# A block-sorted attention feeding a squared-ReLU network: regrouped sorting in the first batch, crossbar transposes for half of the second, and a planner with new due times, new load times and slack behind DMAs

## The chip, the core and the metric

The kernel runs on one core of a Trainium2 chip. The metric is the device time of one execution in microseconds (us), on that one core.

TensorE multiplies matrices, VectorE and ScalarE do elementwise work and empty TensorE's accumulators (PSUM), GpSimd and Sync mostly issue DMAs here. Five instruction streams run side by side and wait for one another by semaphores.

## The reference

Attention over blocks: a softmaxed 8 x 8 matrix P for each head mixes ("sorts") the 8 blocks of keys and values, then each query block attends to its own sorted block of 96 rows. The result, transposed to tokens by features, goes through a two-layer network with squared ReLU.

```python
# batch, heads, seq, head_dim, blocks = 4, 8, 768, 64, 8;  3072 tokens, d_model 512, d_ff 2048
P = sort_net
for _ in range(5):                      # exp, then normalise over rows and columns
    ...
k_sorted = np.einsum('bhij,bhjcd->bhicd', P, k_b).reshape(B, H, S, D)
v_sorted = np.einsum('bhij,bhjcd->bhicd', P, v_b).reshape(B, H, S, D)
...
scores = scale * np.matmul(q_b, k_sb.transpose(0, 1, 2, 4, 3))   # within a block
...                                                              # softmax
attn_out = np.matmul(attn, v_sb).reshape(B, H, S, D)
x = attn_out.transpose(0, 2, 1, 3).reshape(B * S, H * D)
h = np.maximum(x @ w_in, 0.0)
out = h * h @ w_out
```

## The kernel before

The network's matmuls (512 up-projections of 384 columns, 368 down-projections of 512, and a last tile cut in smaller pieces) fill TensorE. The attention of batch b+1 is slipped between the matmuls of batch b. The eight heads of a batch are worked in four pairs.

There are two ways to attention. **On TensorE**: q is transposed by TensorE, k (and in the first batch v) is sorted and transposed in one go by matmuls with a 128-wide expansion of P (`w_all`), and scores are read from `ksT`. **By crossbar DMA**: P is applied in natural layout by quarter-array matmuls (32 x 32, weights `w_t`), VectorE or ScalarE evicts the sorted keys to `kn` in bf16, VectorE copies q, which is bf16 already, to `qi` in another order, and two transposing DMAs on the Sync queue turn them into `kx` and `qT`. Sorted values go out to a DRAM buffer (`v_way`) and come back as `vblk` in the layout that attention-times-values wants. Before the change the first and second batch took the first way for keys and the third and fourth the second; values go by `v_way` from the second batch on.

The order of all instructions is found when the program is built. A planner simulates the engines with a fixed cost for each operation, lets an attention group go ahead of the network's matmuls once its **due time** (counted in chunks of four network matmuls) has come, and emits instructions in the order of the simulated start times. Its estimates never run on the chip; what they fix is the *order* in each engine's queue.

```python
class Plan:
    TAIL = {"PE": 0.0, "ACT": 0.09, "DVE": 0.06, "POOL": 0.0, "DMA": 0.0, "SP": 0.0, "WAY": 0.6}
    HOP = 0.06
    SWITCH = 0.1
    ...
    def ready(self, op):
        if any(d.end is None for d in op.deps):
            return None
        return max([d.end + self.HOP for d in op.deps], default=0.0)
```

"DMA" stands for the loads, whose estimated time is their megabytes over a rate; "WAY" for transfers issued by Sync (the value round trip and the transposes).

```python
    def dma(key, mb, dst_src, deps=()):
        ...
        op = plan.add("POOL", 0.75, issue, deps)
        landed[key] = plan.add("DMA", mb / (0.39 if key[0] == 0 else 0.43), lambda e: None, [op, landed.get("last")])
        landed["last"] = landed[key]
...
    def s_nat(b, g, t, due):            # sort two pairs in natural layout, t = 1 keys, 2 values
        ...
        wr = plan.add("SP", 0.33, write, evs + ([loaded(b)] if b > 1 else []))    # v_way <- vn
        slow = 6.0 if b == 1 else 2.0
        there = plan.add("WAY", slow, lambda e: None, [wr])
        rd = plan.add("SP", 0.33, read, [there] + oldw)                           # vblk <- v_way
        back = plan.add("WAY", slow, lambda e: None, [rd])
...
    def loaded(b):
        return landed[b, 0, HP, 0]      # the last q half of batch b
```

A store of the result is no operation of its own in the plan: it is emitted with the copy that it waits for, so the plan doesn't know that it holds the Sync queue until that copy is done.

```python
            def store(e, mt=mt):
                ob = ffn.tile([128, d_model], FP32, tag="ob", name="ob", bufs=3)
                copy(e, ob, t["op", mt])
                nc.sync.dma_start(out=out[t0 + 128 * mt:t0 + 128 * (mt + 1), :], in_=ob)

            op = plan.add(AD, cost_f(d_model), store, [pe])
```

The softmax here doesn't subtract the row's maximum and nothing guards it: scores larger than these inputs give would overflow.

## Time and profile before

| | before |
|---|---|
| time, median of 3 runs | 226.1 us (226.03 to 226.43) |
| span of the profiled run | 224.2 us, clock 1.0 |
| TensorE busy | 97% |
| VectorE, ScalarE busy | 46%, 54% |
| first up-projection starts | 22.13 us |
| last matmul group ends | 220.29 us |

TensorE sets the time, so the reading is a sum along TensorE: when the network starts, how much work there is, how many changes of array layout, and what is lost in waits. The prediction below does this sum. Three lines from the list of waits: engine, tile and line, then what ended the wait, the total in us, how often, and the longest.

```profile
DVE qi L708 <- DMA qb<-in_q_dram: 7.9, 2, 6.6
...
DVE kn L194 <- DMA kx<-kn: 5.0, 1, 5.0
...
DVE qi L708 <- DMA qT<-qi: 3.1, 2, 2.7
```

VectorE stood 7.9 us before q copies whose load had not landed, and 8.1 us before `kn` and `qi` buffers that a transpose had not freed. A line of a timeline gives start, duration, operation, destination and source, count. The second is the Sync queue's timeline in the fourth batch (start, duration, operation, destination and source, count):

```profile
126.61 3.79 SPq L867 DMA_DIRECT2D out_dram<-ob  x2
141.67 0.38 SPq L668 DMA_DIRECT2D v_way<-vn  x1
142.14 1.66 SPq L696 DMA_TRANSPOSE kx<-kn  x1
143.85 1.39 SPq L719 DMA_TRANSPOSE qT<-qi  x1
145.44 0.43 SPq L867 DMA_DIRECT2D out_dram<-ob  x1
146.53 0.33 SPq L674 DMA_DIRECT2D vblk<-v_way  x1
```

The values are written at 141.67 and read back from 146.53, and the next store comes after the write.

### The profile page before, as it was taken

What the parts mean: (1) busy time and instruction counts of PE and PEld (TensorE: products, weight loads), DVE (VectorE), ACT (ScalarE), POOL (GpSimd) and SP (SyncE); (2) the same over time, 40 slices, a digit from 0 to 9 for tenths busy, and PEclk for the clock granted to TensorE, in tenths of its full rate; (3) what the DMA queues carried; (4) which work ended last, traced back from release to release, by engine and by line L of the source; (5) the groups of instructions that cost most, each with busy time, mean ns of one, the idle gap of its engine ahead of it and who ended that gap; (6) DMA issues with size and microseconds to landing.
All of it is one profiled execution on the core that took longest, in us unless ns stands there. A gap on an engine that the chain in (4) does not pass through costs nothing.

```text
span 224.2 us, 5181 instructions
## 1 busy us (share of the span) xinstructions
PE 216.7 (97%) x2097; PEld 120.5 (54%) x2097; DVE 102.6 (46%) x300; ACT 120.4 (54%) x252; POOL 26.6 (12%) x49
## 2 busy tenths in 40 slices
PE   8998999999999999999999999999999999999993
PEld 2576655546665555445665454436665465456562
DVE  6777777422575416530663236332663255015300
ACT  4666677418985138445765178336772276147421
POOL 7972320000001500000000150000000000000000
PEclk9999999999999999999999999999999999999999
DMA  5999999999221899997922489999843310120012
GB/s 73 202 203 206 208 206 212 209 230 268 59 38 35 146 241 210 137 230 186 144 59 38 129 139 229 198 226 237 192 39 82 83 50 0 47 94 3 0 68 72
DMA packets 43767, 30.43 MB, mean 136 GB/s; under 512 B 22816, under 2 KB 38944, under 8 KB 43744
## 3 DMA queue, kind: packets, MB, share of 16 engines
q0 software_dynamic: 13120, 13.63, 37.3%
q1 hardware_dynamic: 30624, 16.48, 34.0%
q8 instruction: 16, 0.26, 0.5%
q14 instruction: 7, 0.06, 0.1%
HBM read 29.70 MB, written 8.72 MB: 171 GB/s over the span
## 4 chain that ended last, share of the span: by engine, by line
PE 64%; DMA 13%; DVE 9%; issue 5%; ACT 4%; POOL 2%; POOLq 0%; SPq 0%; ACTq 0%; DVEq 0%
PE hp L823 27%; PE op L851 24%; DMA qb<-in_q_dram 8%; DVE ao L755 3%; PE p L561 3%; DMA xT<-ao 3%; PE p L744 2%; DMA kx<-kn 2%; ACT h L831 2%; PE op L885 2%; PE p L644 1%; PE p L518 1%; ACT et L593 1%; PE vbp L609 1%; PE tp L518 1%
## 5 line engine op out<-in xcount | busy, mean ns | idle before, releaser
L823 PE MATMUL hp<-xT,w_in_bf 128*128 128x384 bf16 x512 | 90.7, 327 | 0.5 <-ACT h L831 0.5
L851 PE MATMUL op<-w_out_bf,h 128*128 128x512 bf16 x368 | 83.6, 379 | 0.0
L831 ACT ACTIVATE h<-hp 128x384 bf16<-128x384 f32 x128 | 60.6, 497 | 22.1 <-PE hp L823 15.2
L834 DVE TENSOR_TENSOR h<-h 128x384 bf16<-128x384 bf16 x128 | 43.7, 354 | 54.9 <-ACT h L831 54.0
L823 PEld LDWEIGHTS <-w_in_bf 128*128 128x128 bf16 x512 | 47.2, 97 | 31.6 <-issue 1.4
L851 PEld LDWEIGHTS <-h 128*128 128x128 bf16 x368 | 34.5, 98 | 39.3 <-issue 0.7
L192 ACT COPY ob<-op 128x512 f32<-128x512 f32 (+1 forms) x23 | 13.0, 567 | 58.3 <-PE op L851 52.8
L755 DVE TENSOR_TENSOR ao<-p,rec 96x512 bf16<-96x512 f32 x32 | 22.0, 686 | 1.1
L593 ACT ACTIVATE et<-p 96x384 bf16<-96x384 f32 x48 | 19.5, 492 | 4.8 <-PE p L561 4.8
L744 PEld LDWEIGHTS <-et 96*128 96x128 bf16 x256 | 10.7, 97 | 2.8 <-ACT et L584 0.2
L754 DVE RECIPROCAL rec<-p 96x8 f32<-96x8 f32 x32 | 6.3, 198 | 10.7 <-PE p L744 9.3
L998 POOL COPY held<-xT 1x3 bf16<-1x3 bf16 (+1 forms) x2 | 0.4, 183 | 91.3 <-DMA xT<-ao 91.3
L357 PE MATMUL p<-ones 128*128 128x512 bf16 (+1 forms) x36 | 9.8, 395 | 1.1 <-DVE ones L213 1.1
L744 PE MATMUL p<-vblk,et 96*128 96x65 bf16 x192 | 8.3, 193 | 0.0
L194 DVE CAST kn<-p 128x768 bf16<-128x768 f32 x4 | 3.8, 957 | 8.8 <-DMA kx<-kn 5.0
L708 DVE COPY qi<-qb 128x768 bf16<-128x768 bf16 x8 | 2.7, 355 | 11.0 <-DMA qb<-in_q_dram 7.9
L194 DVE CAST vn<-p 128x768 bf16<-128x768 f32 x6 | 5.7, 957 | 3.3 <-PE p L644 3.3
L264 POOL DMA_DIRECT2D kb<-in_k_dram x10 | 6.6, 662 | 3.6 <-DMA w_in_bf<-in_moe_w_in_dram 2.0
L264 POOL DMA_DIRECT2D qb<-in_q_dram x8 | 6.1, 767 | 4.6 <-DMA w_in_bf<-in_moe_w_in_dram 1.9
L584 ACT ACTIVATE et<-p 96x768 bf16<-96x768 f32 x8 | 6.3, 802 | 0.6 <-PE p L561 0.5
L264 POOL DMA_DIRECT2D vb<-in_v_dram x10 | 6.3, 634 | 2.0 <-DMA w_in_bf<-in_moe_w_in_dram 2.0
L561 PEld LDWEIGHTS <-kx 64*128 64x128 bf16 x128 | 4.6, 155 | 2.9 <-issue 2.9
(81 smaller groups left out, 126.5 us busy)
## 6 DMA issues: line engine op xcount, KB each, us to landing
out_dram<-ob SPq DMA_DIRECT2D x23, 256.0 KB, 3.3
qb<-in_q_dram POOLq DMA_DIRECT2D x8, 384.0 KB, 11.7
v_way<-vn SPq DMA_DIRECT2D x6, 396.0 KB, 5.0
vblk<-v_way SPq DMA_DIRECT2D x6, 396.0 KB, 4.3
vb<-in_v_dram POOLq DMA_DIRECT2D x6, 384.0 KB, 12.5
kb<-in_k_dram POOLq DMA_DIRECT2D x6, 384.0 KB, 10.4
w_in_bf<-in_moe_w_in_dram POOLq DMA_DIRECT2D x4, 512.0 KB, 11.7
w_out_bf<-in_moe_w_out_dram POOLq DMA_DIRECT2D x4, 512.0 KB, 18.8
```

Of the source, the lines that this page charges most:

```text
L192: nc.scalar.copy(out=out, in_=in_)
L194: nc.vector.tensor_copy(out=out, in_=in_)
L264: nc.gpsimd.dma_start(out=dst, in_=src)
L357: nc.tensor.matmul(out=out, lhsT=ones, rhs=rhs, start=True, stop=True)
L561: nc.tensor.matmul(out=scp[:, h, BLK * n:BLK * (n + 1)], lhsT=(u.ksT[64 * h:64 * (h + 1), HS * hf + BLK * n:HS * hf + BLK * n + 128] if u. ...
L593: nc.scalar.activation(out=et[:, h, 0:HS].rearrange("p (n c a) -> p n c a", c=C0, a=NA), in_=st["p"][0:96, h, 0:HS].rearrange("p (n a c) - ...
L744: nc.tensor.matmul(out=oup[:, h, 66 * n:66 * n + D + 1], lhsT=et_r[u.et[hf]][:, h, BLK * n:BLK * n + 128], rhs=(u.vs[:, NQ * hf + n, h, 0: ...
L755: nc.vector.tensor_tensor(out=u.ao[:, n0:n0 + NQ, :, :].rearrange("p n e d -> p e n d"), in0=ov[:, :, :, 0:D], in1=rec[:, :, :, None].to_b ...
L823: nc.tensor.matmul(out=t["hp", nt][:, 0:HS], lhsT=w_in_bf[:, kc, 128 * nt:128 * (nt + 1)], rhs=xT[:, kc, t0:t0 + HS], start=(kc == 0), sto ...
L831: nc.scalar.activation(out=t["h1", nt], in_=t["hp", nt][:, 0:HS], func=AF.Relu)
L834: nc.vector.tensor_tensor(out=t["h2"][:, nt, :], in0=t["h1", nt], in1=t["h1", nt], op=ALU.mult)
L851: nc.tensor.matmul(out=t["op", mt], lhsT=t["h2"][:, nt, 128 * mt:128 * (mt + 1)], rhs=w_out_bf[:, nt, :], start=(nt == 0), stop=(nt == NT ...
```

## The change

Its intent: less TensorE work in the second batch, fewer changes of array layout in the first, and q copies that no longer block VectorE.

1. In the second batch, pairs 2 and 3 take the crossbar way; pairs 0 and 1 stay on TensorE.
2. In the first batch's second half, one function sorts keys and values of a pair into one PSUM tile, with one wide eviction, and due times bring two pairs at a time.
3. Due times of all stages come from a search (table `DUES`) in place of formulas. The planner gets new load times (`rate`, and 4.5 us in place of 3.2 after the hold), 2.5 us of slack behind every load and 1.0 behind every Sync transfer after 45 us ("late landings"), and four `kn` and four `qi` buffers in place of three and two.

```diff
+DUES = {
+    (0, "K"): (-15.0, -1.0, 10, 10),
+    (0, "S"): (-1.0, 11.0, 11.0, 15.0),
 ...
+    (3, "A"): (149.5, 155.0, 160.5, 162.5),
+    (3, "X"): (158.5, 160.0, 161.5, 166.5),
+}
 ...
+    SLACK = {"DMA": 2.5, "WAY": 1.0}
 ...
-        return max([d.end + self.HOP for d in op.deps], default=0.0)
+        late = op.engs[0] not in self.SLACK
+        return max([d.end + self.HOP + (self.SLACK.get(d.eng, 0.0) if late and d.end > 45 else 0.0)
+                    for d in op.deps], default=0.0)
 ...
-    rkx, rkn, rqi = Ring(3), Ring(3), Ring(2)
+    rkx, rkn, rqi = Ring(3), Ring(4), Ring(4)
 ...
-        landed[key] = plan.add("DMA", mb / (0.39 if key[0] == 0 else 0.43), lambda e: None, [op, landed.get("last")])
+        landed[key] = plan.add("DMA", mb / (0.39 if key[0] == 0 else 0.43 if long else rate), lambda e: None, [op, landed.get("last")])
 ...
+    def in_tiles(b, t, h0):
+        return b > 1 and t > 0 or b == 1 and t == 2 or b == 1 and t == 1 and h0 == HP
 ...
+            b < 2 and (b < 1 or in_tiles(b, t, h0)), 0.23 if b == 1 else 0.37 if t else 0.29)
 ...
+    def s_sort2(u, due):
+        ...                       # keys and values of a pair into one PSUM tile
+        u.k_op = u.v_op = plan.add(AD, cost_f(2 * n), ev, pes + u.old)
 ...
-        landed["last"] = plan.add("DMA", 3.2, lambda e: None, [holds[b]])
+        landed["last"] = plan.add("DMA", 4.5, lambda e: None, [holds[b]])
```

More of the change, by code (lines that the diff above doesn't have):

```diff
@@ L13 @@
 AX = mybir.AxisListType
+DUES = {
+    (0, "K"): (-15.0, -1.0, 10, 10),
+    (0, "S"): (-1.0, 11.0, 11.0, 15.0),
+    (0, "T"): (-1.5, 10.0, 13.5, 19.5),
+    (0, "A"): (14.0, 14.5, 18.0, 21.5),
+    (0, "X"): (16.0, 23.0, 24.5, 25.0),
+    (0, "W"): (1.5,),
+    (1, "V"): (4.0, 20.5),
+    (1, "Q"): (31.0,),
+    (1, "N"): (None, 33.0),
+    (1, "Z"): (None, None, 43.0, 44.0),
+    (1, "S"): (33.5, 41.0, 43.0, 48.0),
+    (1, "A"): (39.5, 41.5, 45.5, 52.0),
+    (1, "X"): (48.0, 49.5, 49.5, 55.0),
+    (2, "L"): (52.0,),
+    (2, "N"): (64.0, 69.5),
+    (2, "V"): (74.5, 91.5),
+    (2, "Z"): (84.0, 86.0, 95.5, 96.5),
+    (2, "S"): (88.5, 93.0, 97.5, 100.5),
+    (2, "A"): (95.0, 99.5, 102.0, 104.0),
+    (2, "X"): (96.5, 105.5, 107.5, 109.5),
+    (3, "L"): (110.5,),
+    (3, "N"): (120.0, 126.0),
+    (3, "V"): (123.0, 141.5),
+    (3, "Z"): (130.5, 138.0, 153.0, 155.5),
+    (3, "S"): (143.5, 153.0, 157.5, 159.5),
+    (3, "A"): (149.5, 155.0, 160.5, 162.5),
+    (3, "X"): (158.5, 160.0, 161.5, 166.5),
+}
 FIRST = ("K0 V0 K1 v1 S0 t0 S1 k2 t1 A0 V2 S2 K3 t2 A1 V3 X0 A2 S3 t3 x1 A3 X2 x3")
@@ L215 @@
     nc.vector.memset(ident, 0.0)
-    ksT_r, vsT_r, et_r, vs_r = [], [], [], []
+    kvT_r, et_r, vs_r = [], [], []
     for n in range(3):
-        for r, name in ((ksT_r, "ksT"), (vsT_r, "vsT")):
-            sT = const.tile([128, S + 32], BF16, name=f"{name}{n}")
-            for x in (HS, S):
-                nc.vector.memset(sT[:, x:x + 32], 0.0)
-            r.append(sT)
+        sT = const.tile([128, 2, S + 32], BF16, name=f"kvT{n}")
+        for x in (HS, S):
+            nc.vector.memset(sT[:, :, x:x + 32], 0.0)
+        kvT_r.append(sT)
         vs = const.tile([96, NB, 2, 66], BF16, name=f"vs{n}")
@@ L236 @@
     v_way = nc.dram_tensor("v_way", (B, 2, NA, 128, HP * 66), BF16, kind="Internal").ap()
-    kn_r = [const.tile([128, NA, 2, D], BF16, name=f"kn{n}") for n in range(3)]
-    qi_r = [const.tile([128, NA, 2, D], BF16, name=f"qi{n}") for n in range(2)]
+    kn_r = [const.tile([128, NA, 2, D], BF16, name=f"kn{n}") for n in range(4)]
+    qi_r = [const.tile([128, NA, 2, D], BF16, name=f"qi{n}") for n in range(4)]
     kx_r = []
@@ L259, with dma @@
     landed = {}
-    def dma(key, mb, dst_src, deps=()):
+    def dma(key, mb, dst_src, deps=(), long=True, rate=0.23):
         def issue(e):
@@ L277, in dst_src @@
             alloc_qkv(b)
-            if b > 1 and t or b == 1 and t == 2:
+            if in_tiles(b, t, h0):
                 return (qkv[b][t].rearrange("p (g h) x -> p g (h x)", h=HP)[:, h0 // HP, :],
@@ L282, in load @@
         dma((b, t, h0, p.start), 1.57 * n / H * (p.stop - p.start) / 128, dst_src,
-            readers[b - 2] + [holds[b]] if b > 1 else [])
+            readers[b - 2] + [holds[b]] if b > 1 else [],
+            b < 2 and (b < 1 or in_tiles(b, t, h0)), 0.23 if b == 1 else 0.37 if t else 0.29)
     def load_w_in(g):
@@ L444, in __init__ @@
             self.b, self.hp, self.halves = b, hp, halves
-            if b > 1:
+            self.tiled = in_tiles(b, 1, HP * (hp // 2))
+            if self.tiled:
                 self.i0, self.ni, self.full = 0, NB, True
@@ L448, in __init__ @@
             self.n, self.old = rks.take()
-            self.ksT, self.vsT, self.vs = ksT_r[self.n], vsT_r[self.n], vs_r[self.n]
+            self.kvT, self.vs = kvT_r[self.n], vs_r[self.n]
+            self.ksT, self.vsT = self.kvT[:, 0, :], self.kvT[:, 1, :]
             self.i0, self.ni = NQ * halves[0], NQ * len(halves)
@@ L543, in s_sort, with mm, ev @@
         return op
+    def s_sort2(u, due):
+        st = {}
+        s2, old = r2.take()
+        n = NA * u.ni * C0
+        def mm(e, t):
+            for a in range(NA):
+                for h in range(2):
+                    nc.tensor.matmul(
+                        out=p2[s2][64 * h:64 * (h + 1), t - 1, u.ni * C0 * a:u.ni * C0 * (a + 1)],
+                        lhsT=qkv[u.b][t][:, 2 * u.hp + h, D * a:D * (a + 1)],
+                        rhs=w_all[:, H * u.b + 2 * u.hp + h, u.i0:u.i0 + u.ni, :]
+                        .rearrange("p i c -> p (i c)"),
+                        start=True, stop=True)
+        def ev(e):
+            copy(e, u.kvT[:, :, BLK * u.i0:BLK * (u.i0 + u.ni)]
+                 .rearrange("p t (x a) -> p t x a", a=NA),
+                 p2[s2][:, :, 0:n].rearrange("p t (a x) -> p t x a", a=NA))
+        pes = [plan.add("PE", 0.2, lambda e, t=t: mm(e, t),
+                        [landed[u.b, t, 2 * u.hp, 0], built[H * u.b + 2 * u.hp],
+                         built[H * u.b + 2 * u.hp + 1]] + old, due, mode="col") for t in (1, 2)]
+        readers[u.b] += pes
+        u.k_op = u.v_op = plan.add(AD, cost_f(2 * n), ev, pes + u.old)
+        r2.use(s2, *pes, u.k_op)
     def s_sc(u, due=0):
@@ L555, in mm @@
                 qT = tiles["qT", u.b, u.hp]
-                if u.b < 2:
+                if not u.tiled:
                     qT = qT.rearrange("p a x -> p (a x)").rearrange("p (i q) -> p i q", q=BLK)
@@ L563, in mm @@
                             lhsT=(u.ksT[64 * h:64 * (h + 1), HS * hf + BLK * n:HS * hf + BLK * n + 128]
-                                  if u.b < 2 else
+                                  if not u.tiled else
                                   kx_r[u.kx][64 * h:64 * (h + 1), NQ * hf + n::NB]),
-                            rhs=(qT[64 * h:64 * (h + 1), NQ * hf + n, :] if u.b < 2 else
+                            rhs=(qT[64 * h:64 * (h + 1), NQ * hf + n, :] if not u.tiled else
                                  qT[64 * h:64 * (h + 1), :, C0 * (NQ * hf + n):
@@ L572, in s_sc @@
             u.et[hf], olde = ret.take()
-            pe = plan.add("PE", 0.17 if u.b < 2 else 0.26, mm, [u.k_op, u.q_op] + old, due,
+            pe = plan.add("PE", 0.17 if not u.tiled else 0.26, mm, [u.k_op, u.q_op] + old, due,
                           mode="row")
@@ L576, in s_sc @@
             rqT.use(qTs[u.b, u.hp], pe)
-            if u.b < 2:
+            if not u.tiled:
                 rks.use(u.n, pe)
@@ L946 @@
     todo = []
-    kops = {}
-    def lay(b, halves, c0, c1):
-        step, gap = (c1 - c0) / (HP + 0.9), (c1 - c0 - 13) / (HP - 1)
-        for hp in range(HP):
-            c = c0 + step * hp
-            box = {}
-            def open_(due, b=b, hp=hp, box=box):
-                u = box["u"] = Unit(b, hp, halves)
-                u.q_op = q2ops[hp] if b == 0 else s_q(b, hp, 0, 128, due)
-                if b == 1:
-                    build_w(H * b + 2 * hp, 2, pt, kops[b - 1, hp])
-                u.k_op = kops[b, hp] = s_sort(u, 1, due)
-                if b == 0:
-                    u.v_op = s_sort(u, 2, due)
-            if b == 1 and hp % 2 == 0:
-                todo.append((14 + 2 * hp, len(todo),
-                             lambda due, g=hp // 2: s_nat(1, g, 2, due), b))
-            for f, s in ((0.0, open_),
-                         (0.35, lambda due, box=box: s_sc(box["u"], due)),
-                         (0.5, lambda due, box=box: b == 0 and s_vt(box["u"], due)),
-                         (0.75, lambda due, box=box: s_av(box["u"], due)),
-                         (1.2, lambda due, box=box: s_xt(box["u"], due))):
-                todo.append((c + step * f, len(todo), s, b))
@@ L975, in lay_late @@
-    def lay_late(b, c0):
-        todo.append((c0, len(todo), lambda due: load_late(b), 0))
-        for g in range(2):
-            for t in (1, 2):
-                todo.append((c0 + 9 + 9 * g, len(todo),
-                             lambda due, g=g, t=t: s_nat(b, g, t, due), b))
-        for hp in range(HP):
-            box = {}
-            def scores(due, hp=hp, box=box):
-                u = box["u"] = Unit(b, hp, (0, 1))
-                u.kx, u.k_op, u.q_op = s_turn(b, hp)
-                s_sc(u, due)
-            c = c0 + 25 + 6 * hp
-            todo.append((c, len(todo), scores, b))
-            todo.append((c + 3, len(todo), lambda due, box=box: s_av(box["u"], due), b))
-            todo.append((c + 3, len(todo), lambda due, box=box: s_xt(box["u"], due), b))
@@ L995, in load_late, with sort_first @@
-    def load_late(b):
+    units = {}
+    stages = {"S": lambda b, hp, due: s_sc(units[b, hp], due),
+              "T": lambda b, hp, due: s_vt(units[b, hp], due),
+              "A": lambda b, hp, due: s_av(units[b, hp], due),
+              "X": lambda b, hp, due: s_xt(units[b, hp], due),
+              "V": lambda b, g, due: s_nat(b, g, 2, due),
+              "N": lambda b, g, due: s_nat(b, g, 1, due)}
+    def sort_first(b, hp, due):
+        u = units[0, hp] = Unit(0, hp, (1,))
+        u.q_op = q2ops[hp]
+        s_sort2(u, due)
@@ new lines, in sort_second, with turn, load_late @@
+    def sort_second(b, n, due):
+        for hp in range(2):
+            units[1, hp] = Unit(1, hp, (0, 1))
+            build_w(H + 2 * hp, 2, pt, x_done[0, 2, 1])
+        units[1, 0].q_op = s_q(1, 0, 0, 128, due)
+        for hp in range(2):
+            units[1, hp].k_op = s_sort(units[1, hp], 1, due)
+        units[1, 1].q_op = s_q(1, 1, 0, 128, due)
+    def turn(b, hp, due):
+        u = units[b, hp] = Unit(b, hp, (0, 1))
+        u.kx, u.k_op, u.q_op = s_turn(b, hp)
+    def load_late(b, n, due):
@@ L1005, in load_late @@
                 load(b, t, HP * g, HP)
-    lay(0, (1,), 0, n_up)
-    todo.append((8, len(todo), build_wt, 0))
-    lay(1, (0, 1), n_up, 2 * n_up)
-    lay_late(2, 2 * n_up + 3)
-    lay_late(3, 4 * n_up + 4)
+    stages["K"] = sort_first
+    for (b, name), dues in DUES.items():
+        for n, due in enumerate(dues):
+            fn = {"W": lambda b, n, due: build_wt(due), "L": load_late, "Q": sort_second,
+                  "Z": turn}.get(name) or stages[name]
+            if due is not None:
+                todo.append((due, len(todo), lambda due, fn=fn, b=b, n=n: fn(b, n, due), b))
     for due, _, stage, b in sorted(todo, key=lambda x: x[:2]):
```

## The prediction

> **What bounds the kernel now.** I read the page's engine table and slices first, because they say whether any engine is short of time at all.
>
> ```profile
> PE 216.7 (97%) x2097; PEld 120.5 (54%) x2097; DVE 102.6 (46%) x300; ACT 120.4 (54%) x252; POOL 26.6 (12%) x49
> ...
> PEclk9999999999999999999999999999999999999999
> ```
>
> TensorE is busy 97% of the 224.2 us span at full clock; VectorE and ScalarE stand near half, in bursts. So only three things can save time: less TensorE work, fewer losses between its groups, or an earlier start. The table of costliest groups says what the work is.
>
> ```profile
> L823 PE MATMUL hp<-xT,w_in_bf 128*128 128x384 bf16 x512 | 90.7, 327 | 0.5 <-ACT h L831 0.5
> L851 PE MATMUL op<-w_out_bf,h 128*128 128x512 bf16 x368 | 83.6, 379 | 0.0
> ```
>
> The feed-forward is most of it and the change doesn't touch its counts. The means (327 and 379 ns) are pipelined spans, not costs, so I went to TensorE's timeline and took the distance between starts.
>
> ```profile
> 109.28 2.12 PE L823 MATMUL hp<-xT,w_in_bf 128*128 128x384 bf16 x12
> 111.24 0.66 PE L744 MATMUL p<-vblk,et 96*128 96x65 bf16 x16
> 111.74 2.11 PE L823 MATMUL hp<-xT,w_in_bf 128*128 128x384 bf16 x12
> 113.79 0.71 PE L561 MATMUL p<-qT,kx 64*128 64x96 bf16 x16
> 114.43 1.48 PE L823 MATMUL hp<-xT,w_in_bf 128*128 128x384 bf16 x8
> ...
> 178.56 10.56 PE L823 MATMUL hp<-xT,w_in_bf 128*128 128x384 bf16 x64
> 188.96 10.52 PE L851 MATMUL op<-w_out_bf,h 128*128 128x512 bf16 x48
> 199.32 10.56 PE L823 MATMUL hp<-xT,w_in_bf 128*128 128x384 bf16 x64
> ```
>
> 64 up-projections take 188.96 - 178.56 = 10.40 us, 0.1625 each; 48 down-projections 10.36, 0.2159 each. Twelve up-projections before an attn-times-v group (full array) take 1.96; before a score group (two row halves) they take 2.05. That extra 0.09 to 0.10 recurs at every change of array layout, on the way in and again on the way out. I call it a switch and charge 0.10.
>
> The same subtraction gives per matmul: attn-times-v 0.031, scores on the crossbar keys (kx) 0.033, scores on the TensorE-sorted keys (ksT) 0.0225, sorting matmuls 0.0175 (64 wide) or 0.028 (128 wide), q transposes 0.029, quarter-array key/value sorts (w_t) 0.0138, xT transposes 0.0425, v transposes 0.0565.
>
> From the first up-projection (22.13 us) to the end I count: 512 x 0.1625 = 83.2, 368 x 0.2159 = 79.45, the last tile 3.51, attention 21.67: 187.83 in all. The order has 70 switches, 7.0 us. 22.13 + 187.83 + 7.0 = 216.96, while the trace's last matmul group ends at 216.63 + 3.66 = 220.29. So **3.33 us is lost in waits**, though the wait list gives TensorE hardly any. Going group by group for excess over these costs I find 0.63 (at 80 to 88 us), 0.22 (97.7), 0.68 (139.5), 0.48 (147.7), then 0.22, 0.22 and 0.28 in the first batch (26, 32, 36 us), and 0.09, 0.15, 0.11 elsewhere: 3.08. The two largest, in the timeline of all engines:
>
> ```profile
> 137.79 0.14 PEld L644 LDWEIGHTS <-w_t 32*32 32x32 bf16 x16 [0.32 <-issue]
> ...
> 138.14 0.63 DVE L708 COPY qi<-qb 128x768 bf16<-128x768 bf16 x2 [1.31 <-DMA qb<-in_q_dram]
> ...
> 139.22 0.95 DVE L194 CAST kn<-p 128x768 bf16<-128x768 f32 x1
> 139.51 0.11 PEld L644 LDWEIGHTS <-w_t 32*32 32x32 bf16 x9 [0.32 <-issue]
> 139.51 0.35 PE L644 MATMUL p<-vb,w_t 32*32 32x384 bf16 x8
> 140.00 0.80 ACT L192 CAST vn<-p 128x768 bf16<-128x768 f32 x1
> 140.09 0.62 DVE L834 TENSOR_TENSOR h<-h 128x384 bf16<-128x384 bf16 x2
> 140.23 0.35 PE L644 MATMUL p<-vb,w_t 32*32 32x384 bf16 x8 [0.36 <-DVE kn L194]
> ...
> 147.23 0.96 DVE L194 CAST kn<-p 128x768 bf16<-128x768 f32 x1 [4.98 <-DMA kx<-kn]
> ```
>
> VectorE sat before a q copy whose data had not landed; the squares and the key eviction behind it ran late, so the value matmuls found no free PSUM tile. At 147 the key eviction waited for a transpose to free one of only three kn buffers.
>
> **What the Trainium skill says.** "TensorEngine Tiling (Array Packing)", Key Properties: a change of tiling mode drains TensorE. The trace agrees: the weight load at 137.79 could not run ahead (0.32 us idle), and a switch costs 0.10 us. "Perfetto Trace Analysis", Tensor Engine Instruction: the profiler's matmul end is an estimate, while ScalarE and VectorE are strict FIFO; hence I use starts, and the blocked copy at 138.14 shows the FIFO. "DMA: Bandwidth & Descriptors", DMA Transpose (X-bar): 2-byte data only, issued from Sync or Scalar. Here it needs the bf16 copy qi, 1.2 to 2.3 us on the Sync queue and a median 4.0 (q) or 4.7 us (k) to landing. "Trainium Kernel Development and Optimization", Key Constraints: all queues share the same 16 DMA engines. That agrees with q loads taking 8.7 to 21.0 us to land, by how much is queued.
>
> **The change part by part.** I compared the built instruction order of both kernels.
>
> 1. Second batch, pairs 2 and 3. Gone: 24 q transposes (0.70), 24 128-wide key sorts (0.67), 32 scores on sorted keys (0.72) = 2.09. Added: 16 quarter-array key sorts (0.22), 32 scores on kx (1.06) = 1.28. Net **-0.81 us of TensorE work**. Evictions about cancel: two 768-wide ksT casts become two kn casts of the same size, two qT copies (0.55 to 0.80) become two qi copies (0.35). Sync gains four transposes, four at about 1.3 us.
> 2. Grouping. First batch's second half now sorts k and v into one PSUM tile, two pairs in succession, with one wide eviction per pair, and scores two pairs at once; v moves away from k. Switches after the first up-projection fall from 70 to 58: **-1.2 us**.
> 3. Slack. q copies stand later in VectorE's order (third batch: after 13 squares of its first FFN half; before: the copy had idled 6.6 us and came before nearly all of them), and kn and qi have four buffers instead of three and two. This aims at the 0.63 + 0.22 + 0.68 + 0.48 = 2.01 us of waits. Shifting before's landings by when their loads would now be released puts each of those landings before its copy, one (the last q half of the fourth batch) by under 1 us. I take all 2.01 off.
> 4. The first 22 us: TensorE's order is the same up to the first up-projection, so nothing.
>
> Without waits the new order ends at 22.13 + 187.02 + 5.8 = 214.95. The metric stands 226.1 - 220.29 = 5.8 above the last matmul group's end, which is store and launch, so 220.8 is the floor. Left over: the 1.3 us of waits which part 3 doesn't address (3.33 - 2.01). I expect them to change place rather than vanish, and add 0.2 for tighter bunching: 214.95 + 1.5 + 5.8 = **222.3 us**, 1.7% less.
>
> **Rivals.** *ScalarE takes over in the bunches.* In the third batch the new order packs scores, 8 up-projections, attn-times-v and 8 more up-projections where before had 12 and 12. From the second score group to the third pair's values, 6.6 us by my costs, ScalarE must do 8 exponentials and 7 relus at 0.49 to 0.50, about 7.4. For it: before already lost 0.11 where only 8 stood between. Against: three buffers of slack absorb some. If nothing absorbs it, about 0.8 us here and as much in batches two and four: 224.5.
>
> *Late transposes in the second batch.* Its last q half lands at the latest at 31.73 + 21.0 = 52.7, the turns start after the key evictions near 56, and four cost 4 x 1.3 on the Sync queue plus 4.7: done near 65, where I place the first kx scores (64.8). Pair 2 comes first, so it should be ready near 62; but a crossbar slowed by xT transposes could stall it by 1 to 2 us and delay the hold on the next loads: 223.5 to 224.5.
>
> *The waits vanish entirely* because the search also placed the first batch's work well: 220.8, 2.3% less. For it: the last 70 us have no such loss even now. Against: every dense stretch lost something.
>
> **Range and chances.** The floor 220.8 and the full ScalarE rival 224.5 bound it: 220.9 to 224.6. Faster by over 2% means below 221.6, that is waits under 0.8 us in all; I give that 0.28. Slower by over 2% would need over 9 us of new waits: 0.03.
>
> **What would show it.** Right: 32 matmuls fewer, an up-projection start near 22.1, no VectorE idle before qi over 1 us that delays squares, and value sorts of 0.32 us without a gap inside. Wrong on part 2: up-projections beside row or column groups still losing more than 0.10. Wrong on part 3: a kn or qi eviction again waiting on DMA with TensorE idle behind it. The prediction fails low if the first batch's waits vanish, and high if kx or exponentials hold TensorE.

## The result

| | before | after |
|---|---|---|
| median, same rounds | 226.26 us (226.03 to 226.56, 4 runs) | 223.92 us (223.41 to 224.15, 4 runs) |
| ratio | 1 | 0.9893, 95% interval 0.987 to 0.9916 |
| span of the profiled run | 224.2 us | 222.0 us |

A ratio here is the mean time of one kernel's fast runs over that of the other's of the same rounds, so it isn't quite the ratio of the medians. The change makes the kernel 1.1% faster, 1.6 us short of the predicted 222.3 but within the range.

The engine table and the groups that answer to those of before, and one line of a group that the prediction did not watch:

```profile
PE 213.3 (96%) x2049; PEld 120.0 (54%) x2065; DVE 102.8 (46%) x291; ACT 120.8 (54%) x249; POOL 26.5 (12%) x49
...
PEclk9999999999999999999999999999999999999999
...
L893 PE MATMUL hp<-xT,w_in_bf 128*128 128x384 bf16 x512 | 88.9, 326 | 0.0
L921 PE MATMUL op<-w_out_bf,h 128*128 128x512 bf16 x352 | 83.3, 379 | 0.9 <-issue 0.2
...
L814 PE MATMUL p<-vblk,et 96*128 96x65 bf16 x192 | 8.9, 193 | 1.1 <-DMA vblk<-v_way 1.1
```

The weight loads (PEld) tell the true count: 2065, that is 32 fewer than 2097. The 2049 matmuls are short of that because the records of 16 down-projections are missing from this trace (352 in place of 368), so busy time of the two traces must not be subtracted. The means of the network's matmuls are what they were. New is the last line: attention-times-values idled 1.1 us for values coming back from DRAM.

None of the three waits of VectorE that were shown of before is in the list of waits of after. Around 138 us, where before lost 0.68, all engines' timeline now has:

```profile
137.90 0.38 PE L714 MATMUL p<-vb,w_t 32*32 32x384 bf16 x16
138.21 4.49 PE L921 MATMUL op<-w_out_bf,h 128*128 128x512 bf16 x19
...
138.42 0.96 DVE L231 CAST vn<-p 128x768 bf16<-128x768 f32 x1 [0.18 <-PE p L714]
139.29 0.35 DVE L904 TENSOR_TENSOR h<-h 128x384 bf16<-128x384 bf16 x1
139.56 0.62 DVE L778 COPY qi<-qb 128x768 bf16<-128x768 bf16 x2
```

The sixteen value matmuls take 138.21 - 137.90 = 0.31 us without a gap, and the q copy at 139.56 starts without a wait.

The sum along TensorE, by the prediction's own costs, from the trace:

| | before | after | difference | predicted |
|---|---|---|---|---|
| first up-projection starts | 22.13 | 22.48 | +0.35 | 0 |
| work from there | 187.83 | 187.02 | -0.81 | -0.81 |
| switches at 0.10 | 70: 7.0 | 58: 5.8 | -1.2 | -1.2 |
| waits (the rest) | 3.33 | 2.90 | -0.43 | -1.83 |
| last matmul group ends | 220.29 | 218.20 | -2.09 | -3.84 |

So the shortfall against the prediction is 1.40 us of waits and 0.35 of start. Going group by group, as in the prediction, I find 2.75 of the 2.90 (the rest is the last tile, which this account leaves out; the same account of before, done once more with the built order beside the trace, gives 3.18). All waits given for the experiments below are by this account. The largest in after is 1.24, in TensorE's timeline of the fourth batch:

```profile
152.76 0.70 PE L631 MATMUL p<-qT,kx 64*128 64x96 bf16 x16
153.39 2.77 PE L893 MATMUL hp<-xT,w_in_bf 128*128 128x384 bf16 x16
157.23 0.66 PE L814 MATMUL p<-vblk,et 96*128 96x65 bf16 x16 [1.06 <-DMA vblk<-v_way]
```

Sixteen up-projections at 0.1625 are 2.60, so TensorE was free at 155.99 and stood until 157.23. The Sync queue's timeline says why:

```profile
124.34 22.34 SPq L937 DMA_DIRECT2D out_dram<-ob  x4
146.82 0.38 SPq L738 DMA_DIRECT2D v_way<-vn  x1
147.30 1.62 SPq L766 DMA_TRANSPOSE kx<-kn  x1
149.44 1.22 SPq L789 DMA_TRANSPOSE qT<-qi  x1
...
152.72 0.52 SPq L744 DMA_DIRECT2D vblk<-v_way  x1
```

The value write begins at 146.82, 5.15 us later than before, directly behind the fourth of four stores. Its data were ready long before: the values were evicted by 139.4 (the `vn` cast above). The plan also puts the write behind the last q half (`loaded(b)` in the code above), which was issued by GpSimd at 129.25 and took 13.7 us to land, so it was there at 142.95. That condition only orders the plan. On the chip the write doesn't wait for it: in before the write went out at 141.67, while that half, issued at 131.22 with 13.8 us to landing, was there at 145.0. The line of four stores hides the pause: the third ended at 142.81, and the fourth began at 146.36. What the fourth waited for is in ScalarE's timeline:

```profile
145.75 0.58 ACT L229 COPY ob<-op 128x512 f32<-128x512 f32 x1 [1.89 <-PE op L921]
```

The copy of the output tile ended at 145.75 + 0.58 = 146.33; until then the store held the queue. The Trainium skill, "Perfetto Trace Analysis", DMA Instruction - HWDGE, draws it so: the issuing sequencer itself sits out the semaphore wait, and only the time after it is in the profile. The trace agrees: the fourth store's own bar is 0.33 us, yet nothing was issued on Sync between 142.81 and it. The chain of waits, followed back from the end, passes through the round trip (start, duration, what):

```profile
152.68 0.02 SPq L744
152.69 0.03 issue
152.72 4.46 DMA vblk<-v_way
157.19 0.04 issue
157.23 0.66 PE p L814 x16
```

The other waits of after are small: 0.38 at 40 to 43 us (the second batch's second value sort, whose load lands late), 0.24 at 65.8 and 0.20 at 111.45 (kx scores that need a PSUM tile which VectorE is still normalising), 0.22 at 92.2, and four of 0.09 to 0.15. The 0.22 stands where values are sorted right behind keys.

### The profile page after: what moved, and what is told of

It reads as the page before. It is cut to its first block, busy times and chain, and to the rows that moved or that the text cites. A ratio compares the mean times of both kernels' runs of the same rounds, so it can differ in the third digit from the quotient of the medians.

```text
span 222.0 us, 5101 instructions
## 1 busy us (share of the span) xinstructions
PE 213.3 (96%) x2049; PEld 120.0 (54%) x2065; DVE 102.8 (46%) x291; ACT 120.8 (54%) x249; POOL 26.5 (12%) x49
## 4 chain that ended last, share of the span: by engine, by line
PE 75%; DMA 17%; POOL 4%; ACT 1%; issue 1%; DVE 1%; SPq 0%; ACTq 0%
PE op L921 33%; PE hp L893 31%; DMA vb<-in_v_dram 9%; DMA w_in_bf<-in_moe_w_in_dram 5%; PE p L631 3%; PE p L814 3%; DMA vblk<-v_way 2%; PE op L955 2%; PE p L714 2%; POOL vb L300 1%; POOL kb L300 1%; DMA p_sb<-in_sort_net_dram 1%; ACT h L901 1%; DVE h L904 1%; PE qtp L511 0%
## 5 line engine op out<-in xcount | busy, mean ns | idle before, releaser
L893 PE MATMUL hp<-xT,w_in_bf 128*128 128x384 bf16 x512 | 88.9, 326 | 0.0
L904 DVE TENSOR_TENSOR h<-h 128x384 bf16<-128x384 bf16 x128 | 44.5, 356 | 62.7 <-ACT h L901 62.3
L901 ACT ACTIVATE h<-hp 128x384 bf16<-128x384 f32 x128 | 61.6, 495 | 19.1 <-PE hp L893 15.6
L893 PEld LDWEIGHTS <-w_in_bf 128*128 128x128 bf16 x512 | 48.1, 98 | 32.1 <-issue 1.0
L229 ACT COPY ob<-op 128x512 f32<-128x512 f32 (+1 forms) x24 | 13.6, 567 | 62.4 <-PE op L921 59.8
L814 PEld LDWEIGHTS <-et 96*128 96x128 bf16 x256 | 11.3, 97 | 5.5 <-issue 1.7
L814 PE MATMUL p<-vblk,et 96*128 96x65 bf16 x192 | 8.9, 193 | 1.1 <-DMA vblk<-v_way 1.1
L631 PEld LDWEIGHTS <-kx 64*128 64x128 bf16 x160 | 6.1, 156 | 3.9 <-issue 3.7
L631 PE MATMUL p<-qT,kx 64*128 64x96 bf16 x160 | 7.4, 228 | 0.0
L231 DVE CAST kn<-p 128x768 bf16<-128x768 f32 x5 | 4.8, 957 | 4.8 <-PE p L714 4.8
```

The source lines that it names most:

```text
L229: nc.scalar.copy(out=out, in_=in_)
L231: nc.vector.tensor_copy(out=out, in_=in_)
L631: nc.tensor.matmul(out=scp[:, h, BLK * n:BLK * (n + 1)], lhsT=(u.ksT[64 * h:64 * (h + 1), HS * hf + BLK * n:HS * hf + BLK * n + 128] if no ...
L814: nc.tensor.matmul(out=oup[:, h, 66 * n:66 * n + D + 1], lhsT=et_r[u.et[hf]][:, h, BLK * n:BLK * n + 128], rhs=(u.vs[:, NQ * hf + n, h, 0: ...
L893: nc.tensor.matmul(out=t["hp", nt][:, 0:HS], lhsT=w_in_bf[:, kc, 128 * nt:128 * (nt + 1)], rhs=xT[:, kc, t0:t0 + HS], start=(kc == 0), sto ...
L901: nc.scalar.activation(out=t["h1", nt], in_=t["hp", nt][:, 0:HS], func=AF.Relu)
```

## The experiments

All twelve runs were timed in five rounds beside the kernel before (its medians: 226.22, 225.98 and 226.08, each on another chip), and all results were correct. My theory at this point: the grouping and the crossbar pairs do what the prediction says, and the slack, meant for q copies, put the fourth batch's value write behind a store. Rivals: the wait is chance, or the slack is needed and something else costs more.

### The changed kernel again

No edit. It asks how much is chance.

> The changed kernel, unaltered. It tells how much of its result is chance. Both theories: 223.9 us, within 0.3. In its first trace the first up-projection began at 22.48 us, against 22.13 before, because the q load that the first transposes wait for landed 0.45 us later (transposes from 6.60 instead of 6.15). If that is chance, the start here lies anywhere between 22.1 and 22.5; if it comes with the changed kernel, it is 22.4 to 22.5 again. The wait of 1.24 us before the fourth batch's first attn-times-v group should be there again.

Measured: 224.19 us (223.92 to 224.96, 6 runs), ratio 0.9915 (0.9895 to 0.9935). The late values are there again, larger:

```profile
154.69 1.46 PE L893 MATMUL hp<-xT,w_in_bf 128*128 128x384 bf16 x8
157.89 0.66 PE L814 MATMUL p<-vblk,et 96*128 96x65 bf16 x16 [1.73 <-DMA vblk<-v_way]
```

TensorE was free at 154.69 + 8 x 0.1625 = 155.99 and waited 1.90. Waits are 3.49 in all. The wait is no chance; its size varies by some 0.7 us. The first up-projection started at 22.39, again later than in before, so the expectation's question about the start isn't settled by this run.

### The value write exempt from slack

```diff
-        late = op.engs[0] not in self.SLACK
+        late = op.engs[0] not in self.SLACK and not op.tight
 ...
         wr = plan.add("SP", 0.33, write, evs + ([loaded(b)] if b > 1 else []))
+        wr.tight = True
```

> Only the write of the sorted values to DRAM (v_way) is exempted from the added slack, which puts it one store earlier in the Sync queue in the fourth batch; TensorE's order stays, but for one score group moved by two chunks. Theory: the 1.24 us wait of TensorE for vblk is caused by the Sync queue, where the write stood behind a store that itself waited for a down-projection; it goes, and nothing takes its place: 222.7 us (1.2 less than the changed kernel, ratio to before 0.984). Rival 1: the DMA engines are full at that time, so the values land as late: 223.9. Rival 2: the transposes of k and q now stand behind the write, and the first score group waits instead: 223.2 to 223.5.

Measured: 222.68 us (222.49 to 223.39, 4 runs), ratio 0.9851 (0.9828 to 0.9873), 1.5 us below the unaltered kernel on the same chip. Sync and TensorE in the same places:

```profile
124.27 18.47 SPq L939 DMA_DIRECT2D out_dram<-ob  x3
142.83 0.39 SPq L739 DMA_DIRECT2D v_way<-vn  x1
146.28 0.34 SPq L939 DMA_DIRECT2D out_dram<-ob  x1
...
148.48 0.33 SPq L745 DMA_DIRECT2D vblk<-v_way  x1
```

```profile
154.62 1.47 PE L895 MATMUL hp<-xT,w_in_bf 128*128 128x384 bf16 x8
155.93 0.66 PE L816 MATMUL p<-vblk,et 96*128 96x65 bf16 x16
```

The write now goes before the fourth store, 4 us earlier, and the values' matmuls follow the up-projections at once (154.62 + 1.30 = 155.92). Waits fall from 3.49 to 1.79. The edit exempts the value writes of all batches, but the built orders hardly differ: on Sync only this write, its read and one read in the third batch (from 100.37 to 98.96) change places; on TensorE one score group goes behind 8 more up-projections, and the values' matmuls still come after the same 32. The order of these two DMAs is the cause, and the theory held in its number too.

### Slack and buffers alone, on the kernel before

The kernel before with four `kn` and four `qi` buffers and with the slack, nothing else.

```diff
+    SLACK = {"DMA": 2.5, "WAY": 1.0}
 ...                                    # and ready() as in the change
-    rkx, rkn, rqi = Ring(3), Ring(3), Ring(2)
+    rkx, rkn, rqi = Ring(3), Ring(4), Ring(4)
```

> The kernel before with four kn and four qi buffers (instead of three and two) and the slack for late landings, and nothing else of the change. Its TensorE work is that of before, its order has 74 switches instead of 70 (+0.4 us). Theory: the waits of 0.63, 0.22, 0.68 and 0.48 us that followed from blocked q copies and kn evictions go (1.8 to 2.0): 226.2 - 1.8 + 0.4 = 224.8. Rival: the q copy off the path frees nothing, since the value round trip or the transposes end the wait instead: 226.0 to 226.6.

Measured: 227.98 us (227.16 to 228.82, 6 runs), ratio 1.0073 (1.0045 to 1.0101): slower than before. This missed by 3 us. The order has 74 switches, waits are 5.5, and the largest is the same one as in after:

```profile
153.25 2.12 PE L826 MATMUL hp<-xT,w_in_bf 128*128 128x384 bf16 x12
157.32 0.65 PE L747 MATMUL p<-vblk,et 96*128 96x65 bf16 x16 [1.95 <-DMA vblk<-v_way]
```

TensorE was free at 153.25 + 12 x 0.1625 = 155.20, and waited 2.12. So part 3's gain, as the prediction explained it, isn't to be had from slack and buffers alone, as long as the value writes carry the slack too.

### The grouping undone

The first batch's second half sorts keys and values apart, with the due times that before had.

```diff
-    (0, "K"): (-15.0, -1.0, 10, 10),
-    (0, "S"): (-1.0, 11.0, 11.0, 15.0),
+    (0, "K"): (0.00, 5.71, 11.43, 17.14),
+    (0, "S"): (2.00, 7.71, 13.43, 19.14),
 ...                                     # T, A, X, W and (1, "V") likewise
-        s_sort2(u, due)
+        u.k_op = s_sort(u, 1, due)
+        u.v_op = s_sort(u, 2, due)
```

> The changed kernel with the first batch's second half put back: k and v sorted into two PSUM tiles with two evictions, one pair at a time, at the due times of before. 64 switches instead of 58. Theory: +0.6 us for the switches and +0.4 to 0.7 for the waits on PSUM tiles that before had at 26, 32 and 36 us: 224.9 to 225.2. Rival (the first batch's grouping is hidden, its losses are made up later): 223.9 to 224.1.

Measured: 225.23 us (224.57 to 225.61, 6 runs), ratio 0.9955 (0.9935 to 0.9974), 1.0 above the unaltered changed kernel on the same chip. It has 64 switches (six more, 0.6) and waits of 3.92 against 3.49 (0.43 more, among them the 0.22, 0.23 and 0.27 at 26, 33 and 36 us that the prediction found in before). 0.6 + 0.43 is the 1.0. The grouping is worth that, part of it in waits that I had not credited to it.

### No slack

```diff
-    SLACK = {"DMA": 2.5, "WAY": 1.0}
+    SLACK = {"DMA": 0.0, "WAY": 0.0}
```

> The changed kernel with the slack set to zero; due times, buffers and grouping stay. The fourth batch's value write again stands before the store (as in e1_write_first), but the first two q copies of the third batch stand after about 8 squares instead of 13, and the key sorts come earlier. Theory: the slack is worth something for the q copies and costs something for the value write. So the wait of 1.2 to 1.9 us before the fourth batch's attn-times-v goes, and VectorE waits again 2 to 4 us before qi in the third batch, which costs TensorE 0.5 to 1.5 us behind the squares: 223.2 to 224.0, between e1_write_first (222.7) and the changed kernel (224.2). Rival: the slack does nothing good, and without it the kernel is as fast as e1_write_first: 222.5 to 222.8.

Measured: 222.46 us (222.12 to 222.86, 4 runs), ratio 0.9837 (0.9814 to 0.9861). The write went at 142.98, waits are 1.27, and one q copy waits 1.5 us without TensorE noticing. I had expected the slack to do good for q copies; in this kernel it does none. The changed kernel without it is faster than the version that keeps it for everything but the value write (ratios 0.9837 and 0.9851, whose intervals overlap) and clearly faster than the change as it stands (0.9893 and 0.9915).

### The second batch on TensorE

All four pairs of the second batch on TensorE, in twos, the rest as in the change.

```diff
-    (1, "Q"): (31.0,),
-    (1, "N"): (None, 33.0),
-    (1, "Z"): (None, None, 43.0, 44.0),
+    (1, "Q"): (31.0, 40.0),
 ...
-        return b > 1 and t > 0 or b == 1 and t == 2 or b == 1 and t == 1 and h0 == HP
+        return b > 1 and t > 0 or b == 1 and t == 2
```

> The changed kernel with only the second batch's pairs 2 and 3 put back on TensorE (transposed q, keys sorted by full-width matmuls). TensorE work 187.83 instead of 187.02, 60 switches instead of 58: +1.0 us without waits. Theory: that is what this part is worth, 225.0 to 225.3 against 224.2 for the changed kernel on another chip run. Rival (four transposes more cost as much in waits as they save, by crowding the Sync queue and the loads): 224.0 to 224.4.

Measured: 225.05 us (224.69 to 225.54, 6 runs), ratio 0.9955 (0.9935 to 0.9975), against 0.9893 and 0.9915 for the changed kernel: 0.4 to 0.6% of 226, so 0.9 to 1.4 us. The order has 187.83 us of work (0.81 more) and 60 switches (0.2 more), 1.0 together. The crossbar pairs are worth what step 1 said, and a little in switches.

### Slack and buffers on the kernel before, with the write exempt

The third experiment plus `wr.tight = True`.

> e2_slack_only with the value write exempted from the slack. In e2 TensorE waited 2.12 and 1.57 us in the fourth batch behind late values. Theory: these are the same Sync-queue effect as in the changed kernel; they go, and what the buffers and the slack gain on before's order becomes visible: 228.0 - 3.7 = 224.3, up to 224.8. Rival: other losses stay and the slack gains nothing on before's due times, 226.0 to 226.5.

Measured: 225.16 us (225.07 to 225.42, 6 runs), ratio 0.9959 (0.9939 to 0.9978). Waits fall from 5.5 to 1.96, and the time by 1.1% against the third experiment: the late values were most of what slack cost the kernel before. It lies above the expected 224.3 to 224.8. Against the kernel before it has 1.22 us less in waits and four switches more (0.4), 0.8 us in all, and 0.9 was measured (0.41% of 226). In its trace before's waits of 0.63 and 0.68 behind q copies are gone, and this kernel has the old load times: in before's order slack does keep q copies out of VectorE's way.

### The write exempt, and three due times moved

The second experiment's kernel with the second value sort of the second batch at 22.5, its third scores at 45.4 and the third batch's first value sort at 76.0, each to go after what it waits for.

```diff
-    (1, "V"): (4.0, 20.5),
+    (1, "V"): (4.0, 22.5),
-    (1, "S"): (33.5, 41.0, 43.0, 48.0),
+    (1, "S"): (33.5, 41.0, 45.4, 48.0),
-    (2, "V"): (74.5, 91.5),
+    (2, "V"): (76.0, 91.5),
```

> e1_write_first with three due times moved: the second batch's second value sort two chunks later (it waited 0.39 us for its load and held 0.17 more), the third pair's scores of that batch down (the built order moves only little), the third batch's first value sort one chunk further behind the key sort (0.21). Theory: 0.5 to 0.8 us less than e1_write_first: 221.9 to 222.2. Rival: the values of the second batch come too late for its attn-times-v, and the gain is lost: 222.7 or more.

Measured: 222.6 us (222.46 to 223.16, 4 runs), ratio 0.9848 (0.9825 to 0.9871), no better than 0.9851 without the move: a miss. In the trace the waits did fall, from 1.79 to 1.32, but this run's first up-projection started at 22.66 against 22.22. A gain of half a microsecond is the size of the spread of the start among the changed kernel's variants (22.17 to 22.66).

### More buffers alone, on the kernel before

The third experiment with both slacks at 0.0.

> The kernel before with four kn and four qi buffers, and nothing else (70 switches, work 187.83, no slack). It tells the share of the buffers in the 1.8 us of waits that the change removed. Theory: the buffers take away what came from a full ring, the 0.48 us at 147 and the 0.22 at 97, and leave the two waits behind q copies that wait for a load (0.63 and 0.68): 225.2 to 225.6 against 226.0. Rival 1: buffers alone free all of it, 224.2. Rival 2: they free nothing, 226.0.

Measured: 228.23 us (227.9 to 229.51, 6 runs), ratio 1.01 (1.0073 to 1.0127). None of the theories had this: the buffers alone make the kernel before 1% slower. VectorE's timeline in the third batch:

```profile
83.11 0.63 DVE L711 COPY qi<-qb 128x768 bf16<-128x768 bf16 x2 [6.57 <-DMA qb<-in_q_dram]
...
90.07 0.63 DVE L711 COPY qi<-qb 128x768 bf16<-128x768 bf16 x2 [3.05 <-DMA qb<-in_q_dram]
```

With four `qi` buffers the planner, which believes that loads land sooner than they do, places four q copies early in place of two, and both pairs wait for their load in VectorE's order (13.5 us in all, with the fourth batch). Waits on TensorE are 6.62, against 3.18 in before; the traced run took 229.38, 1.15 above the median, so a usual run has fewer. A buffer more let the wrong estimate do more harm.

### The old load times, without slack

The kernel without slack, with the load times of before.

```diff
-        landed[key] = plan.add("DMA", mb / (0.39 if key[0] == 0 else 0.43 if long else rate), lambda e: None, [op, landed.get("last")])
+        landed[key] = plan.add("DMA", mb / (0.39 if key[0] == 0 else 0.43), lambda e: None, [op, landed.get("last")])
 ...
-        landed["last"] = plan.add("DMA", 4.5, lambda e: None, [holds[b]])
+        landed["last"] = plan.add("DMA", 3.2, lambda e: None, [holds[b]])
```

> e3_no_slack with the planner's load rates and the gap before late loads put back to those of before; due times, grouping and buffers of the changed kernel stay. TensorE's order changes by two chunks in the fourth batch only. Theory: the later landings that the planner reckons with, not the slack, are what moved the q copies behind the squares; without them VectorE waits 2 us and more before qi in the third or fourth batch and TensorE loses 0.5 to 1.5 us: 223.0 to 224.0. Rival: the new due times alone put all early enough out of the way: 222.3 to 222.7.

Measured: 226.83 us (226.44 to 232.34, 6 runs, of which the one at 232.34 was slow, at a clock of 0.947, and is left out of the ratio), ratio 1.0028 (1.0007 to 1.005). That is 4.4 us above the same kernel with the new load times (1.9% by the two ratios), though both have the crossbar pairs, the grouping, the buffers and the searched due times. The wait list has the old wait back, and TensorE pays for it:

```profile
DVE qi L778 <- DMA qb<-in_q_dram: 13.0, 5, 5.0
```

```profile
85.52 1.47 PE L893 MATMUL hp<-xT,w_in_bf 128*128 128x384 bf16 x8
88.09 0.81 PE L893 MATMUL hp<-xT,w_in_bf 128*128 128x384 bf16 x4 [1.10 <-ACT h L901]
89.18 1.46 PE L893 MATMUL hp<-xT,w_in_bf 128*128 128x384 bf16 x8 [0.28 <-ACT h L901]
```

A q copy stands in VectorE's order, the squares behind it run late, ScalarE's relu waits 2.40 us for VectorE at 87.55, and the up-projections wait for the relu. Waits are 6.41, 5.14 more than with the new load times. Of these, the 1.70 between 85.5 and 90.6 shown here and 1.56 before the q transposes at 54.99 stand behind q copies (the copy at 53.30 had waited 4.98 for its load); another 1.47 before 141.57 is TensorE itself at a key sort whose load had not landed. So wrong load times cost in two ways. The direction was expected, the size was not. One reserve: the due times were searched with the new load times, so this pairs old estimates with due times that don't suit them; the 4.4 is what the estimates are worth here, in this order.

### The old buffers, without slack

The kernel without slack, with three `kn` and two `qi` buffers.

```diff
-    rkx, rkn, rqi = Ring(3), Ring(4), Ring(4)
+    rkx, rkn, rqi = Ring(3), Ring(3), Ring(2)
```

> e3_no_slack with three kn and two qi buffers again; TensorE's order stays the same. Theory: the key evictions and q copies wait for transposes again, TensorE loses 0.2 to 0.7 us: 222.7 to 223.2 against 222.5. Rival: with the key and value sorts further apart the old buffers suffice: 222.3 to 222.6.

Measured: 222.39 us (222.13 to 222.85, 4 runs), ratio 0.9837 (0.9814 to 0.986), the same as with four and four. One line of its list of waits:

```profile
DVE qi L778 <- DMA qT<-qi: 16.0, 4, 7.8
```

VectorE waits 16.0 us for `qi` buffers, far more than the 3.1 of before, and TensorE's waits are 1.61 all the same, because the copies now stand where nothing urgent is behind them: after two of the four (at 99.62 and 148.30) VectorE's next instruction waited another 1.83 and 1.49 us for its own input. The rival was right: with this order, the buffers aren't needed.

### No slack, and due times moved

```diff
-    (1, "V"): (4.0, 20.5),
+    (1, "V"): (4.0, 23.2),
-    (1, "S"): (33.5, 41.0, 43.0, 48.0),
-    (1, "A"): (39.5, 41.5, 45.5, 52.0),
+    (1, "S"): (33.5, 41.0, 46.0, 49.0),
+    (1, "A"): (39.5, 41.5, 46.5, 52.0),
-    SLACK = {"DMA": 2.5, "WAY": 1.0}
+    SLACK = {"DMA": 0.0, "WAY": 0.0}
```

> e3_no_slack with two due times of the second batch moved: its second value sort behind two more chunks (it waited for its load, 0.15 and 0.17 us), the third pair's scores one chunk later (0.24 us on a PSUM tile that VectorE was still reading). Theory: 0.3 to 0.5 us less than e3_no_slack: 222.0 to 222.2. Rival: the waits move on, 222.4 to 222.6. The start of the first up-projection has varied by 0.5 us between runs, so the trace (last group less start) decides more sharply than the time.

Measured: 222.01 us (221.9 to 222.28, 4 runs), ratio 0.982 (0.9798 to 0.9841), as expected. Waits are 1.22. It has the lowest median: 1.8% below before, where the change alone brought 1.1%. From the other kernels without slack (0.9837 both) the times don't part it for certain, since the intervals overlap.

## Why the prediction was right or wrong

**Step 1, right in mechanism and size.** The work fell by 32 matmuls, and undoing it cost 0.9 to 1.4 us, where 0.81 of work and 0.2 of switches had to show.

**Step 2, right.** 58 switches, and undoing the first batch's share cost 0.6 in switches and 0.43 in waits. The up-projections beside row and column groups in after lose 0.10, and no more but for the waits listed above.

**Step 3, the step that failed.** "I take all 2.01 off", with 1.5 us of waits left; 2.90 were left. The four named waits did go, with only 0.22 back at 92.2, so the reading of before's trace held. Two things were wrong.

First, what removed them. I credited slack and buffers. Slack can do it: on the kernel before, with the value writes exempt, the waits of 0.63 and 0.68 went, where the buffers alone had left them. But in the changed kernel it wasn't needed: without the slack the waits stayed away too. The buffers are worth nothing with the changed order without slack (222.39 with the old number, 222.46 with the new), and they harm the old one (+1%). What keeps q copies out of VectorE's way there is the planner's better estimate of when loads land, together with the due times searched for it: with the old load times and no slack the kernel took 226.83 in place of 222.46. The diff has these lines, and the prediction doesn't mention them, so that the 2.01 us went as forecast is partly luck. The new load times with the old due times were not tried.

Second, what the slack did besides. The check "Shifting before's landings ... puts each of those landings before its copy" looked at loads and at VectorE's order only. The slack also moves the planned time of a DMA that waits for a load in the plan, and Sync issues in order. In the fourth batch it moved the value write behind a store; the round trip of write and read then ended 1.24 us (1.90 when run again) after TensorE was ready. Exempting the value writes gave 1.5 us. So 1.24 of the 1.40 excess has a cause that an experiment shows. The other 0.16, and most of what was left in small waits, I didn't trace to single causes by experiment.

**Step 4, right about the order, 0.35 us off in the time.** TensorE's order up to the first up-projection is the same, as predicted, but the start came at 22.48 in place of 22.13. Why stays open. In the four traces of before and its variants the start lies at 22.11 to 22.13, in the ten of the changed kernel and its variants at 22.17 to 22.66: 22.48 and 22.39 unaltered, 22.36 without slack, 22.17 with due times moved too. So it varies by half a microsecond among kernels with the same first 22 us, and the slack, which starts only after 45 us, isn't behind it. But no variant of before started late, and one trace of each kernel doesn't show that this is chance. It goes in part with the landing of the first q load: q transposes began at 6.15 in before, 6.60 in after and 6.94 in the run that started at 22.66, but at 6.29 in the one that started at 22.36.

**Three readings.** "The two largest" waits are shown with the 0.68 and the 0.48; the 0.63 at 80 to 88 us was larger than the second. The prediction ties the copy `qi` to the two-byte rule of the transposes, but `qb` is bf16 already (`bf16<-bf16` in the copy's line above); the copy only reorders it. And "8.7 to 21.0 us" for q loads leaves out the first batch's two, at 4.9 and 6.0. None of the three changes the sum.

**The rivals.** ScalarE did not take over: the waits at dense places were for VectorE's normalisation, 0.20 and 0.24. The late transposes in the second batch didn't occur either: issued at 56.5 to 60.6 and landed 2.6 us later each, they were there by 63.1, before the scores at 65.76. I had placed these at 64.8 and the last landing near 65 (with 4.7 us to landing), so the place was sound and the landing reckoned too late. The third rival, that waits vanish, came nearest to true in the versions without slack (1.27 left, 1.22 with due times moved).

**The sum.** 222.3 + 1.40 (waits) + 0.35 (start) is 224.05. The profiled run's time stood 5.55 above the last group's end in place of 5.8, which gives 223.8, and it took 223.75.

## What to carry to other kernels

An order that is fixed when the program is built is as good as the times that the planner believes: correct a wrong transfer time itself, rather than add slack or buffers around it. When a DMA is delayed in the plan, look at what it is queued behind: an in-order queue turns a small delay into the full wait of the instruction ahead. And a wait that is long on an engine with room (16.0 us on VectorE here) costs nothing as long as nothing urgent stands behind it.

## What the Trainium skill lacked or had wrong

- "TensorEngine Tiling (Array Packing)", Key Properties, says that a change of mode drains TensorE but not what it costs. Here it is 0.09 to 0.10 us on the way in and again on the way out; an order with six switches more was 0.6 us longer by this and 0.43 by waits, and 1.0 was measured.
- "DMA: Bandwidth & Descriptors", Rules for kernel authors, advises to issue a DMA early and to wait late. It has no rule on a DMA whose semaphore isn't there yet holding those behind it in the same issuing queue. Here one store did so from 142.81 to 146.36, and putting the value write ahead of it took 1.5 us off 224.19.
- No page gives the time of a round trip through DRAM for a change of layout. Here 396 KB took a median of 4.2 us from issue to landing out and 4.1 back, with 0.38 to 0.52 us on Sync for each in the fourth batch.
- "Perfetto Trace Analysis", Tensor Engine Instruction, does not say that matmul records can be missing. Here 16 of 368 down-projections were, while their weight loads were all recorded, so the change in PE busy time is no measure of the change in work.
- No page says how far a start can vary: the first up-projection came between 22.17 and 22.66 us in ten traces of the changed kernel and its variants, whose first 22 us have the same order on TensorE, and this hid a gain of 0.47 us in one experiment.
